# Blocks of up to 64 tokens with the high and low parts in one stationary operand, and a new order of splits around the transposes of h

## The chip, the cores and the metric

The kernel runs on one core of a Trainium2 chip. The metric is the device time of one execution in microseconds (us). TensorE (PE) multiplies matrices and transposes, VectorE (DVE) and ScalarE (ACT) work on elements, GpSimd (POOL) issues gathers and scatters, SyncE (SP) issues the other transfers. Each engine has an instruction stream of its own, and they meet at semaphores.

## The reference

Three stages follow one another; the change is in the second, which routes each of 1792 tokens to one of 8 experts:

```
def _attn_ref(q, k, v):                      # q, k, v [4, 12, 448, 64]
    scores = scale * np.matmul(q, k.transpose(0, 1, 3, 2)) - np.log(S)
    attn = 1.0 / (1.0 + np.exp(-scores))
    return np.matmul(attn, v)
def _moe_ref(x, expert_emb, tau, w1, w2):    # x [1792, 768], w1 [8, 768, 1024], w2 [8, 1024, 768]
    ...
    for e in range(E):
        mask = expert_idx == e
        h = np.maximum(x[mask] @ w1[e], 0.0)
        out[mask] = gate_w[mask, None] * (h @ w2[e])
def _moe2_ref(x, w_a, w_b, w_out):           # w_a, w_b [768, 1536], w_out [1536, 768]
    return (x @ w_a) * (x @ w_b) @ w_out
```

## The kernel before

The attention of four batches fills PE up to 208 us of the trace, the experts run from there to 545 us, and the last stage (called GLU here) to the end. Everything is float32 in and out. A float32 product is made of three products of parts: each operand is split into a high part, rounded to the narrower type that PE multiplies at full rate, and a low part, the rest; high by high, high by low and low by high are summed in PSUM.

The experts work by blocks of 128 tokens. Tables made on the chip (lines around 343) sort the tokens of two batches at a time by expert, so that there are two phases of 7 blocks each that always run, and then blocks under a condition (`live`, L983). `block(b)` reads a few flags of the next block into registers (`value`, L768): whether the expert changes (`chg`), whether weights are to be loaded (`load`), and which (`e_load`). Where an expert's tokens don't fill their last block, the rest of its rows is computed and thrown away. With this case's inputs 18 blocks do work, seven runs of one expert each with 4, 1, 3, 2, 1, 3 and 4 blocks.

What PE does in a block, in order: `p1_half` for each half `hf` of w1's columns, 6 slices of the 768 inputs by three products (`xh` with `w1h`, `xh` with `w1l`, `xl` with `w1h`, L820 to L822), 36 matmuls of 512 columns; the four transposes of each half of h (`h_tr`, L869), those of the first half inside the second `p1_half`; then 8 slices of h by three products by two halves of the output (`p2`, L906), 48 matmuls of 384 columns, with the transposes of the second half of h behind the first eight and six transposes of the next block's tokens (`x_load`, L756) behind the next four. ACT copies each product to SBUF as `h` with the Relu (L823) and makes the high parts (L760), DVE makes the low parts (L761: `hTl`, `xl`, `w1l`, `w2l`) and the scaled output `y` (L951), which POOL scatters (L957).

Where the expert changes, ACT and DVE also split the new weights under `when_new`, a condition that each of them branches on (L887): w1 in the block before (`split_new(1, 0, KD)`, all six slices behind `x_load`), w2 at that block's end and in the next. SP loads the expert's 7 MB ahead (`load_w`, L772). In the same stretch `prep_tick` makes ready the weights of the GLU: raw words from memory, a copy `ab` on ACT (L199, L201), work on POOL and DVE, and a store `wm<-ab` (L224) on SP; `ab` has three buffers, so that ACT waits there for an earlier store to land.

The order of each engine's instructions is that of the code; buffers come from pools with few tiles (`ps_x` four PSUM tiles for all transposes, `h` two).

## Time and profile before

| | |
|---|---|
| time, median of 3 runs | 1087.31 us (1085.61 to 1088.32) |
| the profiled execution: its time, its span | 1089.07 us, 1087.3 us |
| busy share of the span: PE, DVE, ACT, POOL | 98%, 55%, 46%, 14% |
| the expert stage in the trace | 208.4 to 545.1 us, 18 blocks |
| an ordinary block on PE | 18.0 to 18.1 us |

A share of busy time is a mean over stages; here PE is near full in all three, so a time is read from PE's stream: how long its instructions take, and the few places where it stands.

### The profile page before, as it was taken

What the parts mean: (1) busy time and instruction counts of PE and PEld (TensorE: products, weight loads), DVE (VectorE), ACT (ScalarE), POOL (GpSimd) and SP (SyncE); (2) the same over time, 40 slices, a digit from 0 to 9 for tenths busy, and PEclk for the clock granted to TensorE, in tenths of its full rate; (3) what the DMA queues carried; (4) which work ended last, traced back from release to release, by engine and by line L of the source; (5) the groups of instructions that cost most, each with busy time, mean ns of one, the idle gap of its engine ahead of it and who ended that gap; (6) DMA issues with size and microseconds to landing.
All of it is one profiled execution on the core that took longest, in us unless ns stands there. A gap on an engine that the chain in (4) does not pass through costs nothing.

```text
span 1087.3 us, 16743 instructions
## 1 busy us (share of the span) xinstructions
PE 1066.4 (98%) x5996; PEld 866.6 (80%) x5996; DVE 594.7 (55%) x1037; ACT 501.5 (46%) x761; POOL 152.9 (14%) x218
## 2 busy tenths in 40 slices
PE   7999999999999999999999999999999999999998
PEld 4555555589888988898978878888888888888997
DVE  2566788756792969371255996333334333333553
ACT  5777767442762767261244563332233323233543
POOL 2121322232221222231101331000000000000000
PEclk9999999899999999999999999999999999999999
DMA  6687687639659775823183764073221262220730
GB/s 164 166 214 202 178 234 215 201 110 344 230 211 342 292 254 218 312 62 130 46 285 123 254 209 174 1 290 132 87 87 44 72 273 91 87 88 1 319 132 30
DMA packets 116740, 187.65 MB, mean 173 GB/s; under 512 B 53784, under 2 KB 88856, under 8 KB 110624
## 3 DMA queue, kind: packets, MB, share of 16 engines
q1 hardware_dynamic: 112000, 171.10, 46.8%
q0 software_dynamic: 3040, 14.94, 3.7%
q8 instruction: 48, 0.79, 0.3%
q10 hardware_dynamic: 1600, 0.39, 0.2%
q14 instruction: 52, 0.43, 0.1%
HBM read 154.17 MB, written 32.24 MB: 171 GB/s over the span
## 4 chain that ended last, share of the span: by engine, by line
PE 44%; DVE 3%; DMA 2%; ACT 1%; issue 0%; POOL 0%; SPq 0%; ACTq 0%; POOLq 0%
PE ab L1075 10%; PE ab L1076 10%; PE ab L1077 10%; PE o L1108 5%; PE o L1109 5%; PE o L1110 5%; DVE wlo L761 1%; DMA wx<-wm 1%; DVE m L195 1%; DMA r<-wm 1%; PE ab L756 0%; DVE wx L212 0%; PE py L756 0%; ACT whi L760 0%; DVE m L197 0%
## 5 line engine op out<-in xcount | busy, mean ns | idle before, releaser
L1075 PE MATMUL ab<-yh,whi 128*128 128x512 f32 (+1 forms) x576 | 210.7, 366 | 2.2 <-DVE m L1083 2.1
L1076 PE MATMUL ab<-yl,whi 128*128 128x512 f32 (+1 forms) x576 | 210.0, 365 | 0.0
L1077 PE MATMUL ab<-yh,wlo 128*128 128x512 f32 (+1 forms) x576 | 209.8, 364 | 0.0
L202 POOL TENSOR_TENSOR m<-m,raw 128x384 int32<-128x384 int32 x72 | 76.5, 1063 | 366.2 <-DVE m L197 204.7
L1075 PEld LDWEIGHTS ab<-yh,whi 128*128 128x128 f32 x576 | 109.3, 190 | 18.4 <-DVE m L1083 2.6
L1077 PEld LDWEIGHTS ab<-yh,wlo 128*128 128x128 f32 x576 | 109.4, 190 | 17.5 <-DVE wlo L761 0.2
L1076 PEld LDWEIGHTS ab<-yl,whi 128*128 128x128 f32 x576 | 109.4, 190 | 15.9
L1108 PE MATMUL o<-whi,gh 128*128 128x512 f32 x336 | 114.7, 341 | 0.0
L1109 PE MATMUL o<-whi,gl 128*128 128x512 f32 x336 | 113.8, 339 | 0.0
L1110 PE MATMUL o<-wlo,gh 128*128 128x512 f32 x336 | 112.9, 336 | 0.0
L1083 DVE TENSOR_TENSOR m<-ab,a 128x512 f32<-128x512 f32 (+1 forms) x48 | 29.9, 624 | 146.5 <-PE ab L1077 146.4
L760 ACT CAST gh<-m 128x512 fp32r<-128x512 f32 (+1 forms) x48 | 27.2, 567 | 169.9 <-DVE m L1083 169.9
L557 ACT ACTIVATE a<-ps,bias_s 128x896 f32<-128x896 f32 x96 | 92.8, 1006 | 26.6 <-PE ps L552 25.9
L761 DVE TENSOR_TENSOR wlo<-wx,whi 128x768 fp32r<-128x768 f32 x72 | 65.5, 965 | 49.4 <-ACT whi L760 49.4
L761 DVE TENSOR_TENSOR wlo<-r,whi 128x768 fp32r<-128x768 f32 x70 | 65.1, 985 | 47.9 <-ACT whi L760 47.9
L820 PE MATMUL p<-w1h,xh 128*128 128x512 f32 x216 | 86.3, 399 | 0.1
L821 PE MATMUL p<-w1l,xh 128*128 128x512 f32 x216 | 84.8, 393 | 0.4 <-DVE w1l L761 0.3
L822 PE MATMUL p<-w1h,xl 128*128 128x512 f32 x216 | 84.7, 392 | 0.0
L574 PE MATMUL av<-a,v 128*64 128x448 f32 (+1 forms) x384 | 79.4, 570 | 1.6 <-DVE xtok L590 1.6
L906 PE MATMUL p<-w2h,hTh 128*128 128x384 f32 x288 | 76.5, 346 | 0.0
L760 ACT CAST whi<-wx 128x768 fp32r<-128x768 f32 x72 | 55.4, 832 | 44.2 <-PE o L1109 36.3
L760 ACT CAST whi<-r 128x768 fp32r<-128x768 f32 x70 | 53.8, 832 | 47.0 <-PE o L1109 42.5
(236 smaller groups left out, 1830.2 us busy)
## 6 DMA issues: line engine op xcount, KB each, us to landing
wx<-wm SPq DMA_DIRECT2D x22, 1152.0 KB
r<-wm SPq DMA_DIRECT2D x21, 1152.0 KB
r<-in_moe_w_dram SPq DMA_DIRECT2D x28, 768.0 KB
r<-in_moe_w_dram SPq DMA_DIRECT2D x18, 1024.0 KB
raw<-in_moe_w_a_dram SPq DMA_DIRECT2D x24, 384.0 KB
raw<-in_moe_w_b_dram SPq DMA_DIRECT2D x24, 384.0 KB
raw<-in_moe_w_out_dram SPq DMA_DIRECT2D x24, 384.0 KB
wm<-ab SPq DMA_DIRECT2D x48, 192.0 KB
```

The costliest lines, as they stand in the source:

```text
L557: nc.scalar.activation(out=a[r], in_=ps[:n, :, :S], func=AF.Sigmoid, bias=bias_s[:n], scale=qscale)
L760: nc.scalar.copy(out=hi, in_=src)
L761: eng.tensor_tensor(out=lo, in0=src, in1=f32_hi, op=ALU.subtract)
L820: nc.tensor.matmul(ps, lhsT=xh[:, kk, :], rhs=w1h[kk][:, cs], start=kk == 0, stop=False)
L821: nc.tensor.matmul(ps, lhsT=xh[:, kk, :], rhs=w1l[kk][:, cs], start=False, stop=False)
L822: nc.tensor.matmul(ps, lhsT=xl[:, kk, :], rhs=w1h[kk][:, cs], start=False, stop=kk == KD - 1)
L1075: nc.tensor.matmul(ps[:, :n], lhsT=hi[:, s, cs], rhs=yh[:, kk, :n], start=kk == 0, stop=False)
L1076: nc.tensor.matmul(ps[:, :n], lhsT=hi[:, s, cs], rhs=yl[:, kk, :n], start=False, stop=False)
L1077: nc.tensor.matmul(ps[:, :n], lhsT=lo[:, s, cs], rhs=yh[:, kk, :n], start=False, stop=kk == KD - 1)
L1108: nc.tensor.matmul(t[:, d0:d1], lhsT=gh[:, cs], rhs=hi[:, 2, d0:d1], start=first, stop=False)
L1109: nc.tensor.matmul(t[:, d0:d1], lhsT=gl[:, cs], rhs=hi[:, 2, d0:d1], start=False, stop=False)
L1110: nc.tensor.matmul(t[:, d0:d1], lhsT=gh[:, cs], rhs=lo[:, 2, d0:d1], start=False, stop=last)
```

## The change

A block gets a sixth flag, `full_of`. It is 0 for an expert's second block if the expert has at least three and its remainder is at most 64 tokens; the ranks of its tokens are moved so that the partly filled block is that second one, not the last. In such a half block the low parts of x go into columns 64 to 127 of `xh` behind the high parts of the same 64 tokens, so that one product with `w1h` and one with `w1l` do for both, and the third product is left out. Instead of transposing h on PE, a matmul with the constant `fold` (two identities above each other) sums the two halves of rows while it turns them. The split then puts the high parts of h in columns 0 to 63 of `hTl` too and uses `hTl` as the stationary operand of p2; `y` is summed from the two halves of rows. With these inputs blocks 1 (64 tokens), 6 (3 tokens) and 15 (64 tokens) are half blocks. All engines that differ branch on the flag.

In all blocks after the first: the three products of p1 run one after the other over all slices; the Relu moves from the copy of h to its split; `x_load` comes behind the whole first half of p2 and behind the split of h's second half, with two new slices of w1 split ahead of it and four behind; in the second half of p2 `hTl`'s products stand ahead of those with `w2l`.

```
+    fold = ctile([P, P], "fold")
...
+        for cs in (slice(0, P // 2), slice(P // 2, P)):
+            gp.tensor_tensor(out=fold[:, cs], in0=ident[:, :P // 2], in1=ident[:, P // 2:], op=ALU.add)
...
+        over = st("over", [P, E2])
+        ve.scalar_tensor_tensor(out=over, in0=nb, scalar=-float(P), in1=run, op0=ALU.mult, op1=ALU.add)
...
+        ve.scalar_tensor_tensor(out=over, in0=nb, scalar=-float(P), in1=run, op0=ALU.mult, op1=ALU.add)
+        po = st("po", [CP, MAXC, E], tag="py")[:, :n_c, :]
+        gp.tensor_tensor(out=po, in0=oh_all[:, c0:c1, :],
+                         in1=over[:CP, ph * E:(ph + 1) * E].unsqueeze(1).to_broadcast([CP, n_c, E]), op=ALU.mult)
+        yield
+        yield
+        ov = st("ov", [CP, MAXC], tag="pr")[:, :n_c]
+        ve.tensor_reduce(out=ov, in_=po, axis=AX.X, op=ALU.add)
+        rq = st("rq", [CP, MAXC], tag="bk")[:, :n_c]
+        ve.tensor_tensor(out=rq, in0=rk_all[:, c0:c1], in1=ov, op=ALU.subtract)
+        ve.scalar_tensor_tensor(out=ov, in0=rq, scalar=2.0 * P, in1=ov, op0=ALU.is_ge, op1=ALU.mult)
+        ve.tensor_tensor(out=rq, in0=rk_all[:, c0:c1], in1=ov, op=ALU.subtract)
         ri = st("ri", [CP, MAXC], I32)[:, :n_c]
-        ve.tensor_copy(out=ri, in_=rk_all[:, c0:c1])
+        ve.tensor_copy(out=ri, in_=rq)
...
+        fw = st("fw", [1, E2])
+        ve.tensor_scalar(out=fw, in0=over[0:1], scalar1=-float(P // 2), scalar2=None, op0=ALU.is_le)
+        ve.scalar_tensor_tensor(out=fw, in0=nb[0:1], scalar=3.0, in1=fw, op0=ALU.is_ge, op1=ALU.mult)
+        ve.scalar_tensor_tensor(out=fw, in0=beg[0:1], scalar=2.0, in1=fw, op0=ALU.add, op1=ALU.mult)
...
+        ve.tensor_scalar(out=flg[ph][:, 5, :n_t], in0=hb_, scalar1=-1.0, scalar2=1.0, op0=ALU.mult, op1=ALU.add)
...
+    def either(b, whole, half, who=1):
+        if b not in full_of:
+            whole()
+            return
+        with tc.If(full_of[b][who] == 1) as c:
+            whole()
+        with c.Else():
+            half()
+
+    def x_high(b, hf, px):
+        n = KD // 2
+        src = px[:, :n * P].rearrange("p (k c) -> p k c", k=n)
+        nc.scalar.copy(out=xs_t[b % 2][0][:, hf * n:(hf + 1) * n, :], in_=src)
+        return src
+
+    def x_low(b, srcs):
         xh, xl = xs_t[b % 2]
         n = KD // 2
-        ks = slice(hf * n, (hf + 1) * n)
-        split(xh[:, ks, :], xl[:, ks, :], px[:, :n * P].rearrange("p (k c) -> p k c", k=n), xh[:, ks, :].bitcast(F32))
+
+        def low(o, cs, os):
+            for hf, src in enumerate(srcs):
+                ks = slice(hf * n, (hf + 1) * n)
+                nc.vector.tensor_tensor(out=o[:, ks, os], in0=src[:, :, cs], in1=xh[:, ks, cs].bitcast(F32),
+                                        op=ALU.subtract)
+
+        either(b, lambda: low(xl, slice(0, P), slice(0, P)), lambda: low(xh, slice(0, PH), slice(PH, P)), 2)
...
+            x_low(b, [x_high(b, hf, pxs[hf]) for hf in range(2)])
...
+    def when_full(b, whole, half=None, again=True):
+        if b not in full_of:
+            whole()
+            return
+        with tc.If(full_of[b][0] == 1, label=f"full{b}_{n_full[0]}", preferred_fallthrough_block=True) as c:
+            whole()
+        if half is not None:
+            with c.Else():
+                half()
+        n_full[0] += 1
+        if again:
+            hint(b)
...
+        if b in full_of:
+            def run_over(l, wv, first=False, last=False):
+                for kk in range(KD):
+                    nc.tensor.matmul(ps, lhsT=l[:, kk, :], rhs=wv[kk][:, cs], start=first and kk == 0,
+                                     stop=last and kk == KD - 1)
+
+            run_over(xh, w1h, first=True)
+            if hf == 0:
+                when_full(b, lambda: run_over(xl, w1h))
+            else:
+                px = misc["ps"]()
+
+                def whole():
+                    run_over(xl, w1h)
+                    h_turn(b, 0, px, False)
+
+                when_full(b, whole, lambda: h_turn(b, 0, px, True))
+                h_split(b, 0, px)
+                inner()
+            run_over(xh, w1l, last=True)
...
-        nc.scalar.activation(out=h, in_=ps, func=AF.Relu)
+        nc.scalar.copy(out=h, in_=ps)
...
+    def h_turn(b, hf, px, half):
+        for kk in range(FH // P):
+            cs = slice(kk * P, (kk + 1) * P)
+            if half:
+                nc.tensor.matmul(px[:, cs], lhsT=hs_of[b][hf][:, cs], rhs=fold, start=True, stop=True)
+            else:
+                nc.tensor.transpose(out=px[:, cs], in_=hs_of[b][hf][:, cs], identity=ident)
+
+    def h_split(b, hf, px):
+        n = FH // P
+        hi, lo = (hT[nm][:, hf * n:(hf + 1) * n, :] for nm in "hl")
+        src = px.rearrange("p (k c) -> p k c", k=n)
+        nc.scalar.activation(out=hi, in_=src, func=AF.Relu)
+        nc.vector.scalar_tensor_tensor(out=lo, in0=src, scalar=0.0, in1=hi.bitcast(F32), op0=ALU.max,
+                                       op1=ALU.subtract)
+        if b in full_of:
+            with tc.If(full_of[b][3] == 0):
+                nc.scalar.activation(out=lo[:, :, :PH], in_=src[:, :, :PH], func=AF.Relu)
...
+            def half1(yp, px, half):
+                a = hTl if half else hTh
+                p2(yp, 0, 2, ((a, w2h), (a, w2l)))
+                h_turn(b, 1, px, half)
+
+            def half1b(yp, half):
+                a = hTl if half else hTh
+                p2(yp, 2, KF // 2, ((a, w2h), (a, w2l)))
+                if not half:
+                    p2(yp, 0, KF // 2, ((hTl, w2h),))
+
+            def half2(yp, half):
+                a = hTl if half else hTh
+                p2(yp, KF // 2, KF, ((a, w2h),))
+                if not half:
+                    p2(yp, KF // 2, KF, ((hTl, w2h),))
+                p2(yp, KF // 2, KF, ((a, w2l),))
...
-            p2(yp, 0, 2, slice(0, 2))
-            h_tr(b, 1)
-            p2(yp, 2, 3, slice(0, 2))
+            px = misc["ps"]()
+            when_full(b, lambda: half1(yp, px, False), lambda: half1(yp, px, True))
+            when_full(b, lambda: half1b(yp, False), lambda: half1b(yp, True))
+            h_split(b, 1, px)
+            if b > 0:
+                when_new(lambda: split_new(1, 0, 2))
+            else:
+                split_new(2, 4, KF)
             x_load(b + 1)
             if b == 0:
-                split_new(2, 4, KF)
                 when_new(lambda: load_new(1), load)
                 when_new(lambda: load_new(2), load)
-            when_new(lambda: split_new(1, 0, KD))
-            p2(yp, 3, KF // 2, slice(0, 2))
-            p2(yp, 0, KF // 2, slice(2, 3))
+            when_new(lambda: split_new(1, 2 if b > 0 else 0, KD))
             gather(b + 2)
             tick()
             if 0 < b < LIVE - 1:
                 prep_tick(behind=1)
-            p2(yp, KF // 2, KF, slice(0, 2))
-            p2(yp, KF // 2, KF, slice(2, 3))
+            when_full(b, lambda: half2(yp, False), lambda: half2(yp, True), False)
...
+            def y_half():
+                gt = slots[:, 2, b:b + 1]
+                for hf in range(2):
+                    yo = y[:, hf * HD:(hf + 1) * HD]
+                    nc.scalar.activation(out=yo, in_=yp[hf][:, :HD], func=AF.Copy, scale=gt)
+                    nc.vector.scalar_tensor_tensor(out=yo[:PH], in0=yp[hf][PH:, :HD], scalar=gt[:PH], in1=yo[:PH],
+                                                   op0=ALU.mult, op1=ALU.add)
+
+            either(b, y_whole, y_half)
...
+                full_of[nx] = [value(nx, 5, 1, es) for es in ([ET.PE], [ET.Activation, ET.DVE], [ET.DVE], [ET.Activation])]
```

The order on the engines, at three places of blocks 5 and 6, both in the unrolled code (every block has the same rows). PE in the second `p1_half` of block 5, around the transposes of the first half of h; `p_...` is the accumulator, `xh` and `xl` the parts of the tokens. Before:

```order
L820 MATMUL p_4176<-w1h_123,xh_116 128x512
L821 MATMUL p_4176<-w1l_129,xh_116 128x512
L822 MATMUL p_4176<-w1h_123,xl_117 128x512
L869 MATMUL px<-ident,h 128x128 x4
L820 MATMUL p_4176<-w1h_124,xh_116 128x512
L821 MATMUL p_4176<-w1l_130,xh_116 128x512
```

And with the change:

```order
L888 MATMUL p_4721<-w1h_125,xl_118 128x512
L888 MATMUL p_4721<-w1h_126,xl_118 128x512
L959 MATMUL px<-ident,h 128x128 x4
L873 UNCONDITIONAL_BRANCH
L957 MATMUL px<-fold,h 128x128 x4
L873 UNCONDITIONAL_BRANCH
L989 UNCONDITIONAL_BRANCH
L888 MATMUL p_4721<-w1l_127,xh_117 128x512
```

The transposes stand behind twelve of eighteen matmuls as they did, but what follows them is the six with `w1l`; a full block jumps over the matmuls with `fold`, a half block comes to them with neither the six `xl` products nor the transposes.

ACT from the end of block 5 to the copy of h in block 6 (`flg` holds the flags, `r` the loaded weights). Before:

```order
L201 ACTIVATE ab<-raw 128x384
L887 COMPARE_AND_BRANCH
L760 CAST w2h_2790<-r_2921 128x768
L760 CAST w2h_2791<-r_2921 128x768
L760 CAST w2h_2792<-r_2921 128x768
L760 CAST w2h_2793<-r_2921 128x768
L887 UNCONDITIONAL_BRANCH x2
L768 TENSOR_LOAD flg_105
L768 ISA x2
L823 ACTIVATE h<-p_4368 128x512
```

And with the change:

```order
L1085 ACTIVATE y<-p_4778,slots 128x384
L1085 ACTIVATE y<-p_4779,slots 128x384
L820 UNCONDITIONAL_BRANCH
L989 COMPARE_AND_BRANCH
L784 CAST w2h_2812<-r_2943 128x768
L784 CAST w2h_2813<-r_2943 128x768
L784 CAST w2h_2814<-r_2943 128x768
L784 CAST w2h_2815<-r_2943 128x768
L989 UNCONDITIONAL_BRANCH x2
L792 TENSOR_LOAD flg_106
L792 ISA x2
```

Here the last two rows stand three times before the copy of h comes; ahead of them is a branch around the two `y` operations of a half block.

ACT behind the second half of h in block 5. Before:

```order
L201 ACTIVATE ab<-raw 128x384
L760 CAST hTh<-px 128x512
L760 CAST xh_114<-px 128x384 x2
L887 COMPARE_AND_BRANCH
L760 CAST w1h_120<-r_0_118 128x1024
```

And with the change:

```order
L965 ACTIVATE hTh<-px 128x512
L969 COMPARE_AND_BRANCH
L970 ACTIVATE hTl<-px 128x4x64
L969 UNCONDITIONAL_BRANCH x2
L989 COMPARE_AND_BRANCH
L784 CAST w1h_121<-r_0_119 128x1024
L784 CAST w1h_122<-r_0_119 128x1024
L989 UNCONDITIONAL_BRANCH x2
L828 CAST xh_115<-px 128x384 x2
```

A half block's copy into `hTl` (L970) follows the high part, and the tokens' high parts come behind two slices of w1.

## Rows read from the trace of the kernel before

**Rows 1.** The page: busy time by engine, and the chain that ended last.

```profile
PE 1066.4 (98%) x5996; PEld 866.6 (80%) x5996; DVE 594.7 (55%) x1037; ACT 501.5 (46%) x761; POOL 152.9 (14%) x218
...
PE 44%; DVE 3%; DMA 2%; ACT 1%; issue 0%; POOL 0%; SPq 0%; ACTq 0%; POOLq 0%
```

**Rows 2.** Windows, blocks 6, 7, 11, 14: busy time, PE clock, DMA share, GB/s.

```profile
325.10:343.10 18.00, 18.00 (x100) 16.40 (x99) 6.39 (x12) 4.58 (x9) 4.76 (x5) 1.00 1.01 378
...
343.10:362.30 19.20, 18.15 (x99) 16.26 (x98) 9.53 (x13) 10.16 (x15) 3.12 (x4) 1.00 0.58 205
...
416.60:436.80 20.20, 19.20 (x100) 16.04 (x99) 18.80 (x27) 11.89 (x21) 5.31 (x5) 1.00 0.38 128
...
472.80:490.90 18.10, 18.10 (x99) 16.33 (x99) 13.44 (x19) 9.18 (x15) 7.69 (x2) 1.00 0.31 102
```

**Rows 3.** Timeline of PE in block 15: start us, us, engine, line.

```profile
497.55 0.39 PE L822 MATMUL p<-w1h,xl 128*128 128x512 f32 x1
497.78 0.60 PE L869 MATMUL px<-ident,h 128*128 128x128 f32 x4
498.13 0.48 PE L820 MATMUL p<-w1h,xh 128*128 128x512 f32 x1
...
502.17 0.63 PE L756 MATMUL px<-ident_r,xg 128*128 128x128 f32 x6
...
503.40 1.55 PE L906 MATMUL p<-w2h,hTl 128*128 128x384 f32 x8
504.79 0.51 PE L906 MATMUL p<-w2h,hTh 128*128 128x384 f32 x2
```

**Rows 4.** Timeline of PE, plain float32 matmuls of 84 columns.

```profile
267.49 1.02 PE L427 MATMUL px<-hotb,hotp 112*128 112x84 f32 x8
268.30 0.47 PE L820 MATMUL p<-w1h,xh 128*128 128x512 f32 x1
```

**Rows 5.** Timeline of PE at the end of the expert stage.

```profile
545.83 0.42 PE L756 MATMUL py<-ident_r,raw 128*128 128x128 f32 x3 [0.70 <-PEq L983]
```

**Rows 6.** Timeline of ACT in block 15.

```profile
498.46 0.59 ACT L760 CAST hTh<-px 128x512 fp32r<-128x512 f32 x1 [2.55 <-PE px L869]
```

**Rows 7.** Timeline of DVE in block 15.

```profile
499.08 0.69 DVE L761 TENSOR_TENSOR hTl<-px,hTh 128x512 fp32r<-128x512 f32 x1 [6.98 <-ACTq L887]
```

**Rows 8.** Timeline of SP in blocks 6 and 7.

```profile
325.07 1.88 SPq L772 DMA_DIRECT2D r<-in_moe_w_dram  x3
...
340.57 0.34 SPq L224 DMA_DIRECT2D wm<-ab  x1
```

**Rows 9.** Timeline of all engines in block 7.

```profile
349.12 0.55 ACT L201 ACTIVATE ab<-raw 128x384 f32<-128x384 bf16 x1 [9.08 <-DMA wm<-ab]
...
350.48 0.60 ACT L823 ACTIVATE h<-p 128x512 f32<-128x512 f32 x1 [0.82 <-ACTq L887]
...
351.13 0.66 PE L869 MATMUL px<-ident,h 128*128 128x128 f32 x4 [1.05 <-ACTq L887]
```

**Rows 10.** Timeline of ACT in block 9.

```profile
384.99 0.55 ACT L201 ACTIVATE ab<-raw 128x384 f32<-128x384 bf16 x1 [8.83 <-DMA wm<-ab]
386.28 0.60 ACT L823 ACTIVATE h<-p 128x512 f32<-128x512 f32 x1 [0.74 <-ACTq L887]
```

**Rows 11.** Timeline of PE in block 9.

```profile
387.29 0.60 PE L869 MATMUL px<-ident,h 128*128 128x128 f32 x4
```

**Rows 12.** Source line L768, register loads: ns min/median/max, first and last start.

```profile
L768 ACTq TENSOR_LOAD <-flg x23: 272/279/557, 220.6 to 522.4; - x23
...
L768 ACTq FUSED_REGOPS  x18: 147/147/173, 221.2 to 522.2; - x18
```

**Rows 13.** Source line L887, branches of the expert's change.

```profile
L887 ACTq COMPARE_BRANCH  x94: 34/40/141, 224.8 to 539.6; - x94
```

**Rows 14.** Source line L983, branches of the conditional blocks.

```profile
L983 PEldq COMPARE_BRANCH  x6: 63/82/375, 469.7 to 545.5; - x6
```

**Rows 15.** Timeline of DVE in block 5.

```profile
302.80 6.92 DVE L761 TENSOR_TENSOR w1l<-r,w1h 128x1024 fp32r<-128x1024 f32 x6
```

More of the change, by code (lines that the diff above doesn't have):

```diff
@@ L353, in tables @@
         ve.tensor_copy(out=rpf, in_=rp)
-        yield
-        yield
         cum = st("cum", [P, E2])
@@ L804, in x_load, with hint @@
             transpose_raw(pxs[hf], t, hf * n, n)
-            if not first:
-                x_split(b, hf, pxs[hf])
-        for hf in range(2):
-            if first:
-                x_split(b, hf, pxs[hf])
+        if first:
+            for hf in range(2):
+                src = x_high(b, hf, pxs[hf])
+                ks = slice(hf * n, (hf + 1) * n)
+                nc.vector.tensor_tensor(out=xl[:, ks, :], in0=src, in1=xh[:, ks, :].bitcast(F32), op=ALU.subtract)
+        else:
+            x_low(b, [x_high(b, hf, pxs[hf]) for hf in range(2)])
         xT_[b] = (xh, xl)
     e_of, hs_of = {}, {}
+    def hint(b):
+        tc.mark_branch_hint_location(f"full{b}_{n_full[0]}", full_of[b][0], [ET.PE])
+    n_full = [0]
+    def when_full(b, whole, half=None, again=True):
[10 more added lines that the diff above has]
+            hint(b)
     def p1_half(b, hf, ps, h, inner, at=4):
@@ L900, in p1, with p2 @@
                         mx_p.tile([P, FH], F32, tag="h", name="h"), inner)
[L902 removed]
+            def p2(yp, k0, k1, parts):
                 for kk in range(k0, k1):
[L904 removed]
+                    for i, (l, wv) in enumerate(parts):
                         for hf in range(2):
                             nc.tensor.matmul(yp[hf][:, :HD], lhsT=l[:, kk, :], rhs=wv[kk][:, hf * HD:(hf + 1) * HD],
[L907 to L908 removed]
+                                             start=kk == 0 and i == 0 and len(parts) == 2,
+                                             stop=kk == KF - 1 and wv is w2l)
+            def half1(yp, px, half):
[13 more added lines that the diff above has]
+                p2(yp, KF // 2, KF, ((a, w2l),))
             def tick():
```

51 lines of the change are left out of this document (27 added, 24 removed).

## The prediction

> **What bounds the kernel now.** I read the page first: PE is busy 98% of the span and heads the chain that ended last [rows 1]. Next the windows, one for each block [rows 2]: in an ordinary block PE is busy the whole time, 18.00 of 18.00 us in block 6, at a granted clock of 1.00, while DVE and ACT work a third of it. So what a block costs is the sum of PE's matmuls, and a matmul taken out of a block shortens it, unless what PE then comes to sooner isn't there yet. The windows also show where PE stands already: block 7 takes 19.20 us with 18.15 busy, block 11 20.20 with 19.20. The timeline of block 7 shows what the first of these is [rows 9]: PE waited 1.05 us to turn h's first half, since ACT had sat 9.08 us until a store `wm<-ab` had landed, then made `ab` at 349.12, read its registers and copied h at 350.48, so that PE could begin at 351.13 only. This is where I expect part of the gain to be lost. The rest of what I read are prices.
>
> **What a half block leaves out.** On PE two 512-column matmuls start 0.23 us apart (497.55, 497.78), and eight of 384 columns take 504.79 - 503.40 = 1.39 us, 0.174 each [rows 3]. A half block loses 12 matmuls with `xl`, 12 x 0.23 = 2.75 us, and 16 with `hTl` in p2, 16 x 0.174 = 2.78, together 5.5 us.
>
> **What it adds on PE.** Four transposes and what they delay come to 0.45 us: they start at 497.78, the next matmul at 498.13, and that one takes 0.48 where others take 0.39 [rows 3]. A turn with `fold` is a plain float32 matmul; four such, of 84 columns, stand as eight passes from 267.49 to 268.30, 0.81 us [rows 4]. With 128 columns I take 0.9, twice in a block, so +0.9 over the transposes. (Lower end 0.7, at 0.81 a turn; upper end 1.6, if the passes grow with the columns, 0.81 x 128/84 = 1.23.)
>
> **Waits of the half block.** Before `hTl` can be the stationary operand three steps must follow the turn: ACT's high part (498.46, 0.59 us) [rows 6], DVE's low part (499.08, ended 499.77) [rows 7], and ACT's copy of the high half into `hTl`, which no row shows. It has half the elements of a 0.59 us operation; I estimate 0.35 (between nothing but its hand-over, 0.05, and 0.59). From the turn's end at 498.38 [rows 3] to 499.77 + 0.35 and about 0.1 of hand-overs are 1.85 us, and two conditions on ACT are ahead of the copy, each a branch of 0.04 us [rows 13], and a wait of ACT for its own last operation, so I take 2.1. In the first half only six matmuls with `w1l` cover it, 6 x 0.23 = 1.4 us, less what the turn still takes: PE stands 0.8 (0.4 to 1.1). In the second, eight matmuls (1.39) and `x_load`'s six transposes (502.17; half as much again as four, 0.5 or more [rows 3]) do: 0.3 (0 to 0.6). PE's jump from p1 to the first turn also makes it stand. The only taken jump on PE in the trace is the exit of the conditional blocks, where it stood 0.70 us [rows 5], its sequencer's own part at most 0.375 [rows 14]; I take 0.35 (0 to 0.7).
>
> So block 15 gains 5.5 - 0.9 - 1.1 - 0.35 = 3.15 us. Block 1 has the same sum, but about 1 us of small table matmuls lies among its own and covers a part of the first wait: 3.3.
>
> **Block 6's gain is not kept.** It is 3.15 us too, and block 7 follows. The store on which ACT sat had been issued at 340.57, with the expert's loads issued from 325.07 on ahead of it [rows 8], in a block in which the DMA engines were full, share 1.03 [rows 2]. The loads start at block 6's beginning, which its own length doesn't move, so the store still lands at about 349.05. Before block 7 ACT also has two more registers to read, 0.28 + 0.15 us each [rows 12], and a branch around `y` with its jump, together about 1.2 to 1.45 us, all between `ab` and h's copy (in the order shown above they stand just there). So h is turned at about 352.4 where it was at 351.13: block 6's 3.15 are gone and 1.3 more. A little of it is made good by an earlier start of block 6 (below): blocks 5 to 7 together +1.0. Both ends: if the store lands by as much earlier as block 6 is shorter, this term is -2.0 instead; if ACT's extra work is longer, +2.
>
> **Block 9.** The same waiting, without a half block: `ab` 384.99, h's copy 386.28 [rows 10], ends 386.88, and PE turns h at 387.29, not late yet [rows 11]. There are 0.4 us to spare, and ACT's extra 1.3 comes on top: +0.9 (0 to 1.4). In the other blocks ACT comes to h's copy earlier than PE wants it by more than this: nothing there.
>
> **New order in full blocks.** Where the expert changes, the low parts of w1 are what PE comes to too soon: six of them take DVE 6.92 us in one piece [rows 15] in block 5, and block 11, the other of its kind, takes 20.20 us against 18.10 in block 14 [rows 2]. With all `xh` by `w1h` first, then `xl`, the first `w1l` is wanted 12 matmuls (2.7 us) later but all six then in one row, and DVE has two slices done ahead of the tokens: -0.5 for the two blocks (-1.5 to +0.5). The tokens' parts come 2.1 us later (12 matmuls by 0.174), of some 9 us that they have: nothing, unless ACT and DVE are as full as in those blocks, which is the upper end.
>
> **Branches on PE in full blocks.** Each has five compares and four jumps over at most 26 instructions. A compare on PE takes 0.06 to 0.08 us of its sequencer [rows 14], on ACT 0.04 [rows 13], the jumps among them at most 0.141. PE's sequencer is about 3 us ahead of its matmuls (the compare ahead of block 14 is at 469.7 [rows 14], that block begins at 472.80 [rows 2]), so a delay of this size is made good before a matmul is late: +0.5 for all 14 blocks, for stops that don't quite fit. The low end is 0. What it costs if that cover is gone is the slower rival.
>
> The extra table operations (ten small ones on DVE and POOL) lie beside PE's work in blocks 0 to 6; attention and GLU keep their instructions: 0.
>
> **The sum.** -3.15 - 3.3 + 1.0 + 0.9 - 0.5 + 0.5 = -4.5 us. The profiled execution took 1089.07 us and so would come to 1084.5; the median of the runs is 1.76 lower, and from it 1087.31 - 4.5 = 1082.8, my forecast.
>
> **The rivals.** *Jumps on PE are paid for (slower).* If the sequencer isn't ahead at a jump, because the jump empties what it had read, every one costs between half and all of the 0.375 us of [rows 14]. 14 full blocks with 4 jumps are 56, +10.5 to +21 us on -5.0: 1093 to 1103. For it speaks the exit, where PE stood 0.70 [rows 5]; against it that the exit leads far, and that these lead over few instructions. The sum turns to slower than now at 5.0/56 = 0.09 us a jump. The Trainium skill, "Runtime: NRT & Kernel Launch", section "Instruction fetch mechanics", says that a taken branch whose target is outside the fetched pages waits for a DMA fetch; jumps over 26 instructions mostly stay within, so by it the sum would be the one without its +0.5, 1082.3. No row here shows which jumps leave the pages.
>
> *Block 6's gain is kept.* The store lands earlier, or another transfer's order lets ACT go: -4.5 - 3.0 = -7.5, 1079.8. For it: less traffic may stand ahead of it; against it the DMA share of 1.03, which leaves no room.
>
> *Nothing is left.* What block 1 gains is lost where a later block waits for a store or for weights, as block 6's is: -4.5 + 3.3 = -1.2, 1086.1; with the waits, the jump and the turns of block 15 at their upper ends too (0.3 + 0.3 + 0.35 + 0.7 = 1.65 more) it is 1087.8. For it: blocks 2 to 5 lie under the same transfers; against it: PE has no wait of a microsecond in them now.
>
> **How the numbers follow.** The sum 0.5; block 6 kept 0.17; nothing left 0.18; jumps paid 0.15. The likeliest alone reaches from 1080.5 to 1086 (turns and waits ±1, order ±1, ACT's extra ±1). The range 1079 to 1091 takes in all but the jumps and the lowest part of block 6 kept, some 0.2. 0.3%, about what a measurement of this kernel can tell from no change, is 3.3 us: faster means below 1084.05. Of the sum 0.31 lies there and 0.19 within, block 6 kept lies below, nothing left within, and of the jumps 0.13 lie above 1090.6 and 0.02 within: faster 0.48, same 0.39, slower 0.13.
>
> **What will show it.** The windows of blocks 1, 6 and 15 should show about 15 us, with 1 to 1.5 of PE idle, waiting in PE's waits for ACT at the first `hTl` product. Block 7 should grow to about 23 us, its transposes waiting for ACT, and block 9 by 0.9. An ordinary full block (8, 12, 16) should stay at 18.0 to 18.1; if it is 18.2 or more, jumps are paid and the forecast fails. If block 7 stays at 19 us, block 6's gain was kept; if blocks 2 to 4 grow by 3 us, block 1's was lost. A block 11 above 20.2 would put the order of the splits wrong.

## The result and the profile after

The changed kernel takes 1094.74 us (1092.48 to 1095.58, 6 runs) beside 1087.82 of the kernel before on the same chip: ratio 1.0066, with a 95% interval of 1.005 to 1.0082. It is slower by 7 us; I had forecast 4.5 us faster, and the time is outside my range. The profiled execution is its fastest, 1092.48 us with a span of 1090.8, and that of the kernel before, 1089.07 us, is slower than all six runs timed here, so the traces show 3.5 us of the 7.

The page after, busy time. PE works 10.3 us less than before [rows 1] in a longer span.

```profile
PE 1056.1 (97%) x5936; PEld 855.6 (78%) x5936; DVE 601.4 (55%) x1059; ACT 508.4 (47%) x773; POOL 155.0 (14%) x222
```

The windows of blocks 1, 2, 5, 6, 7, 9, 13 and 15 of the kernel after, columns as in [rows 2]:

```profile
228.91:244.47 15.56, 15.05 (x89) 13.42 (x89) 8.33 (x30) 6.13 (x13) 4.32 (x9) 1.00 0.22 63
244.47:265.20 20.73, 19.32 (x107) 17.29 (x107) 16.94 (x57) 5.76 (x11) 6.82 (x11) 1.00 1.03 398
...
303.20:323.95 20.75, 19.36 (x98) 16.30 (x99) 19.15 (x28) 12.09 (x21) 4.02 (x4) 1.00 0.34 118
323.95:345.96 22.01, 16.49 (x79) 14.65 (x79) 6.50 (x12) 5.44 (x11) 5.01 (x5) 0.85 1.01 377
345.96:364.65 18.69, 18.37 (x100) 16.48 (x99) 9.27 (x13) 11.19 (x17) 3.78 (x3) 0.99 0.42 136
...
383.19:401.20 18.01, 18.01 (x99) 16.43 (x99) 9.14 (x13) 10.13 (x15) 4.44 (x4) 1.00 0.48 164
...
457.94:477.04 19.10, 18.24 (x99) 16.36 (x99) 7.82 (x10) 9.21 (x13) 3.33 (x3) 1.00 0.22 80
...
495.60:510.50 14.90, 14.08 (x80) 12.24 (x80) 3.55 (x6) 4.00 (x8) 1.95 (x2) 1.00 0.37 127
```

Blocks 1 and 15 gave 3.4 and 3.1 us (they take 15.56 and 14.90). Block 6, half as well, takes 22.01 us of which PE works 16.49, at a clock of 0.85; before it took 18.00 [rows 2]. Ordinary blocks such as 9 stay at 18.01. Between them blocks 2, 5 and 13 grew by 1.9, 1.1 and 1.1, and 4, 8, 10 and 14 by 0.4 to 0.8. The stage (from the first matmul of block 0 to the last of block 17) took 338.9 us instead of 336.4, and the GLU behind it 540.15 instead of 538.27.

The waits of PE from block 0 to the end of the stage, us in total, how many, the longest (a name with `q` is an engine's sequencer, which takes branches, register loads and semaphores):

```profile
PE p L1008 <- ACTq L989: 6.3, 4, 4.8
...
PE px L959 <- ACT h L911: 1.8, 6, 0.3
PE p L1008 <- DVEq L989: 1.5, 3, 1.0
PE p L888 <- DVE w1l L785: 1.3, 2, 0.6
PE px L959 <- ACTq L989: 1.2, 2, 0.9
```

These name ACT or DVE, none PE's own sequencer; left out are the attention's, those at the way out, and two of 0.4 us and less. The largest is at the first `hTl` product of a half block. The timeline of ACT in block 6 shows it, and PE's row there:

```profile
331.61 0.59 ACT L911 COPY h<-p 128x512 f32<-128x512 f32 x1 [0.18 <-ACTq L989]
...
338.39 0.54 ACT L204 ACTIVATE ab<-raw 128x384 f32<-128x384 bf16 x1 [5.75 <-DMA wm<-ab]
338.84 0.58 ACT L965 ACTIVATE hTh<-px 128x512 fp32r<-128x512 f32 x1
340.24 0.38 ACT L970 ACTIVATE hTl<-px 128x256 fp32r<-128x256 f32 x1 [0.82 <-DVEq L989]
```

```profile
340.68 1.33 PE L1008 MATMUL p<-w2h,hTl 128*128 128x384 f32 x3 [4.79 <-ACTq L989]
```

ACT copied h's second half at 331.61, then stood 5.75 us behind the store `wm<-ab` with the next `ab`, and split h at 338.84 only; DVE's low part and the copy into `hTl` (L970) followed, and PE had stood 4.79 us. PE's clock there, in windows of 4 us:

```profile
336.00:340.00 4.00, 0.00 (x0) 0.00 (x0) 0.54 (x1) 1.03 (x2) 0.98 (x1) 0.92 1.04 403
340.00:344.00 4.00, 3.32 (x10) 3.33 (x11) 2.59 (x6) 1.80 (x4) 0.00 (x0) 0.50 1.03 403
344.00:348.00 4.00, 4.00 (x16) 3.65 (x16) 0.05 (x1) 0.00 (x0) 1.02 (x1) 0.73 0.85 308
348.00:352.00 4.00, 4.00 (x19) 3.31 (x18) 1.15 (x2) 1.61 (x3) 0.00 (x0) 1.00 0.45 143
```

By the means of these rows the granted clock is 0.50, the lower of the two levels (1.2 GHz), from about 339.4, while PE still stands, until about 346.2. PE's work from 340.7 on, 5.5 us, goes at half speed there: an estimated 2.8 us lost behind the 4.8.

The same comes once more at the way out of the stage. Timeline of the first products and parts of the GLU:

```profile
548.55 1.69 ACT L784 CAST yh<-py 128x384 fp32r<-128x384 f32 x4 [5.46 <-DVEq L1119]
...
551.25 1.95 DVE L785 TENSOR_TENSOR yl<-py,yh 128x384 fp32r<-128x384 f32 x4 [3.56 <-ACT whi L784]
...
552.89 0.76 PE L1212 MATMUL ab<-yh,whi 128*128 128x512 f32 x1 [2.41 <-DVE yl L785]
```

```profile
550.00:552.00 2.00, 0.48 (x6) 0.34 (x4) 0.75 (x2) 2.00 (x6) 0.00 (x0) 0.75 0.93 333
552.00:554.00 2.00, 1.11 (x3) 0.85 (x4) 2.00 (x5) 2.00 (x5) 0.00 (x0) 0.50 1.06 439
554.00:556.00 2.00, 2.00 (x6) 1.56 (x6) 2.00 (x6) 0.13 (x1) 0.00 (x0) 0.50 0.94 355
556.00:558.00 2.00, 2.00 (x6) 1.57 (x5) 2.00 (x5) 1.67 (x3) 0.00 (x0) 0.54 1.11 375
```

ACT's `yh` begins at 548.55 and DVE's last branch out of the conditional blocks is at 548.6, but its first `yl` is at 551.25. PE works 1.6 us of the four from 550 to 554, and the clock is at its lower level from about 551 to 558. Before, too, PE stood at its exit [rows 5], but not for the first `yl`, and its clock fell as well, for half as long:

```profile
548.00:550.00 2.00, 2.00 (x14) 1.77 (x12) 2.00 (x5) 2.00 (x6) 0.00 (x0) 0.50 0.79 181
550.00:552.00 2.00, 2.00 (x7) 1.51 (x7) 2.00 (x6) 1.90 (x5) 0.00 (x0) 0.65 1.07 433
```

### The profile page after: what moved, and what is told of

Its sections match the earlier page's. It is cut to its first block, busy times and chain, and to the rows that moved or that the text cites. A ratio compares the mean times of both kernels' runs of the same rounds, so it can differ in the third digit from the quotient of the medians.

```text
span 1090.8 us, 17515 instructions
## 1 busy us (share of the span) xinstructions
PE 1056.1 (97%) x5936; PEld 855.6 (78%) x5936; DVE 601.4 (55%) x1059; ACT 508.4 (47%) x773; POOL 155.0 (14%) x222
## 4 chain that ended last, share of the span: by engine, by line
PE 43%; DVE 3%; DMA 2%; ACT 1%; issue 1%; POOL 0%; SPq 0%; ACTq 0%; DVEq 0%; POOLq 0%
PE ab L1212 10%; PE ab L1213 10%; PE ab L1214 10%; PE o L1245 5%; PE o L1246 5%; PE o L1247 5%; DMA wx<-wm 1%; DVE wlo L785 1%; DVE m L198 1%; DMA r<-wm 1%; PE ab L780 0%; DVE wx L215 0%; ACT whi L784 0%; DVE m L200 0%; POOL m L205 0%
## 5 line engine op out<-in xcount | busy, mean ns | idle before, releaser
L1214 PEld LDWEIGHTS ab<-yh,wlo 128*128 128x128 f32 x576 | 109.3, 190 | 17.5 <-DVE wlo L785 0.2
L784 ACT CAST whi<-wx 128x768 fp32r<-128x768 f32 x72 | 55.3, 832 | 41.9 <-PE o L1246 35.4
L1245 PEld LDWEIGHTS o<-whi,gh 128*128 128x128 f32 x336 | 63.4, 189 | 8.2
L1246 PEld LDWEIGHTS o<-whi,gl 128*128 128x128 f32 x336 | 63.5, 189 | 7.4
L1247 PEld LDWEIGHTS o<-wlo,gh 128*128 128x128 f32 x336 | 63.2, 188 | 7.4
L1008 PE MATMUL p<-w2h,hTl 128*128 128x384 f32 x288 | 59.8, 344 | 8.1 <-ACTq L989 6.3
```

The source lines that it names most:

```text
L784: nc.scalar.copy(out=hi, in_=src)
L1008: nc.tensor.matmul(yp[hf][:, :HD], lhsT=l[:, kk, :], rhs=wv[kk][:, hf * HD:(hf + 1) * HD], start=kk == 0 and i == 0 and len(parts) == 2, s ...
L1214: nc.tensor.matmul(ps[:, :n], lhsT=lo[:, s, cs], rhs=yh[:, kk, :n], start=False, stop=kk == KD - 1)
L1245: nc.tensor.matmul(t[:, d0:d1], lhsT=gh[:, cs], rhs=hi[:, 2, d0:d1], start=first, stop=False)
L1246: nc.tensor.matmul(t[:, d0:d1], lhsT=gl[:, cs], rhs=hi[:, 2, d0:d1], start=False, stop=False)
L1247: nc.tensor.matmul(t[:, d0:d1], lhsT=gh[:, cs], rhs=lo[:, 2, d0:d1], start=False, stop=last)
```

## The experiments

The kernel before was timed again beside each group of runs and came to between 1085.46 and 1087.82 us. Kernels of different groups are therefore compared by what each takes over its own before; the kernel after takes 6.9 us over it.

**What the parts cost: all blocks whole, and the order alone.**

```diff
 # all_full
-        ve.tensor_scalar(out=flg[ph][:, 5, :n_t], in0=hb_, scalar1=-1.0, ...
+        ve.tensor_scalar(out=flg[ph][:, 5, :n_t], in0=hb_, scalar1=0.0, ...
```

> The sixth flag is always 1: every block is computed whole, with all branches, register loads and table operations of the change; nothing of the output changes. Theory A (the full blocks pay on ACT's and DVE's queues: register loads, conditions, later operands): the time is that of the change plus the work that blocks 1 and 15 had saved (3.4 + 3.1 us) less the wait of 4.8 us and the slower blocks 6 and 7 (3.4 us over before): about +3 to +5, 1097.5 to 1100 us, PE's waits naming ACT and DVE, and an ordinary block such as 9, 12, 16 still 18.0 us. Theory B (PE pays at its own branches): the same total, but ordinary blocks at 18.3 us or more. Theory C (the half blocks themselves lose, by their waits): it is no slower than the change, 1093 to 1095 us or less.

1099.43 us, ratio 1.0117 (1.0098 to 1.0137). An ordinary block is 18.00 to 18.04, so theory B falls: PE's branches cost nothing that shows. The stage is 345.07 us, 8.7 over before, in blocks 2, 4 to 8, 10, 13 and 14, and PE's waits there are for ACT and DVE. Theory C falls as well: the half blocks bring something, 6.2 us in the stage, 7.1 by the times over before (14.0 here). But not all of it is kept. The window of block 2 here:

```profile
250.09:269.18 19.09, 19.06 (x108) 17.32 (x107) 15.32 (x54) 4.70 (x9) 5.57 (x9) 1.00 1.03 399
```

Behind a whole block 1, block 2 takes 19.09 us; behind the half block it takes 20.73. So 1.6 of the 3.4 us that block 1 gives come back there. Blocks 6 and 7 take 41.9 us here and 40.7 in the kernel after: what block 6 leaves out brings 1.2.

```diff
 # order_only: no flag, no condition, no register load, the tables of before
-        with tc.If(full_of[b][0] == 1, ...) as c:
-            whole()
+        whole()
...
-                full_of[nx] = [value(nx, 5, 1, es) for es in ...]
+                full_of[nx] = True
```

> The new order of p1, of the splits and of p2 in all blocks, but no flag, no branch, no register load, no half block, and the tables of before; nothing of the output changes. Theory A (register loads and conditions make ACT and DVE late): about the time of before, 1086.5 to 1089 us, blocks 4, 8, 10 at 18.1 and block 13 at 18.0. Theory D (the new order itself is late where weights change): 1090 us or more, with blocks 5 and 11 at 20.5 us and blocks 4, 8, 10, 14 at 18.4 or more, waiting for h's copy.

1091.40 us, ratio 1.005 (1.0031 to 1.0069), 5.9 over its before: slower, so by its time theory D seemed right, but its blocks say no. Blocks 4, 8, 10 and 14 are at 18.14, 13 at 18.02 and the stage at 336.79, before 336.4; blocks 5 to 7 are together 1.2 longer, 0 and 11 shorter. What its trace shows lost is mostly in the GLU, 539.39 us or 1.1 more, where PE waits 2.0 us for the first `yl` as in the kernel after. The conditions and register loads then are what makes blocks 8, 10, 13 and 14 longer in all_full.

**The way out of the blocks.** Idle DVE operations in the code of a block that never runs:

```diff
 # dve_pad
             either(b, y_whole, y_half)
+            if b == NBLK - 1:
+                for _ in range(64):
+                    nc.vector.memset(y[:, 0:1], 0.0)
```

> The change, with 64 tiny DVE operations added to the code of the last conditional block, which never runs here: they only move where the code that follows lies. Theory E (DVE stands 2.1 us at its jump out of the conditional blocks because the code it leads to isn't there yet, which depends on where it lies): the standing before the first yl changes, to 0.2 us or to another place, and the time with it by up to 2 us, 1092.5 to 1095 us. Rival F (DVE waits there for data): the 2.1 us stay, whatever the code's place.

1090.06 us (12 runs), ratio to before 1.0032 (1.002 to 1.0045): 3.7 us over its before where the kernel after takes 6.9, so 3.2 less, though no instruction that runs is different. I had expected 2 at most. Timeline of DVE and of PE there, and a window at its clock:

```profile
550.26 1.95 DVE L785 TENSOR_TENSOR yl<-py,yh 128x384 fp32r<-128x384 f32 x4 [1.58 <-ACT yh L784]
```

```profile
551.89 0.48 PE L1215 MATMUL ab<-yh,whi 128*128 128x512 f32 x1 [0.42 <-DVE yl L785]
```

```profile
552.00:554.00 2.00, 2.00 (x7) 1.28 (x8) 2.00 (x6) 2.00 (x7) 0.00 (x0) 1.00 1.09 433
```

The standing before the first product is 0.42 us instead of 2.41, the clock stays at its upper level, and the GLU takes 536.75 us, 3.4 less: 2.0 of standing, and I put the rest down to the half clock. Rival F falls. Three more kernels tried to say which place is bad:

```diff
 # before_pad: the same loop with range(125) in the kernel before
 # order_pad: range(3) in order_only;  order_pad64: range(64) in it
```

> The kernel before, with 125 tiny DVE operations added to the code of its last conditional block, which never runs here; they move the code that follows on DVE to the place that it has in order_only (instruction 2255 of its stream, not 2130). Theory E (the place of code costs the time at the jump out of the conditional blocks): DVE stands some 2 us between its last jump and the first yl, and the time is 2 to 4 us above before, 1088.5 to 1090.5 us, without a change in any block. Rival F: nothing changes, within 0.5 us of before.

1087.54 us, ratio 1.0005 (0.9992 to 1.0019), 0.40 us of standing: theory E in this form is wrong. The place in DVE's own stream isn't what decides; the rest of the program differs between the two kernels, and so may where the code lies.

> order_only with 3 tiny DVE operations added to the code of the last conditional block, which never runs; the code behind it then lies where it does in the kernel before modulo 128 instructions. Theory E: the 2.2 us of standing before the first yl are gone, the time is 2 to 4 us below order_only, 1087 to 1089.5 us. Theory D (the new order itself costs what order_only lost): unchanged, 1090 to 1092 us.

1091.16 us, 2.03 us of standing, GLU 539.41: as order_only, so theory E fails here too; the time is that of theory D, the blocks are not.

> order_only with 64 tiny DVE operations in the code of the last conditional block, which never runs. If what order_only loses (1091.4) is the standing of 2.0 us at the way out of the blocks and the half clock after it, and 64 operations move it away as they did in dve_pad: no standing over 0.5 us before the GLU's first product, the stage 336.5 to 337 us, the time 1086 to 1088.5 us, that of before. If the new order of p1 and the splits costs by itself: 1090 to 1092 us with the standing gone. If 64 operations don't move it here: the standing of 2 us is seen again and the time is 1090.5 to 1092.

The standing is gone, GLU 538.22, yet 1089.88 us, ratio 1.0028 (1.0016 to 1.0041). Its stage is 336.82. Over their own before order_only takes 5.9 us, order_pad 3.6 and this one 3.1: with the standing went between 0.5 and 2.8 us. The first two differ by three operations that never run, both stand, and yet lie 2.4 us apart, so a difference of 2 us between groups shows little. Of the 3.1 that stay, the stage shows 0.4; the rest is open (below).

**Register loads.**

```diff
 # loads_behind: chg, live and full are read here, no longer ahead of the block
                 p1(0, lambda: None)
+                got = flags()
```

> The change, with the register loads of the flags (the expert's change, live, full) put behind the copy of h's first half of a block instead of ahead of it; nothing of the output changes. Theory A3 (register loads on ACT between a late ab and the copy of h cost time): block 13's wait of 0.86 us and some of block 7's go and ACT stands less before h; 1 to 3 us less than the change, 1092 to 1094 us. Rival: the loads are hidden but for block 13, and the time is within 0.5 us of the change; or they now delay the split of h's first half, and it is slower by 1 us or more.

1093.69 us, ratio 1.0071 (1.0053 to 1.009), 8.2 over its before, so no gain: block 13 came back to 18.03 and 7 to 18.03, but 5, 8, 10, 14 and 15 grew by 0.4 to 1.5. Both theory and rival have a part: the moved loads are late for something else. Its block 6 shows another cost, on PE's timeline:

```profile
329.13 1.30 PE L888 MATMUL p<-w1h,xh 128*128 128x512 f32 x5
335.35 0.98 PE L957 MATMUL px<-fold,h 128*128 128x128 f32 x3 [4.92 <-issue]
```

At the jump of a half block to its first `fold` PE stood 4.92 us for nothing that the profile shows ("issue"), h having been copied long before (ACT, 329.16 to 329.75). In the half blocks of the kernel after it doesn't stand at this jump.

```diff
 # one_flag: ACT and DVE take a block as half where chg is 2
+        ve.scalar_tensor_tensor(out=flg[ph][:, 1, :n_t], in0=hb_, scalar=2.0, in1=c0_[:, :n_t], ...
...
-                full_of[nx] = [value(nx, 5, 1, es) for es in ([ET.PE], [ET.Activation, ET.DVE], ...)]
+                full_of[nx] = [value(nx, 5, 1, [ET.PE]), chg]
```

> The change, with the half block told by the value 2 of the flag of the expert's change, so that ACT and DVE read one register for each block as before, not three; nothing of the output changes. Theory A3 (register loads on ACT and DVE cost time where ACT is late): block 13 back to 18.0 to 18.3 us, block 7 1 us shorter, block 2 0.4 shorter; 2 to 3.5 us less than the change, 1091 to 1093 us. Rival A4 (the conditions around h's split and y cost it, not the loads): within 1 us of the change, with the 0.3 us waits for h's copy in blocks 4, 8, 10, 14 as they are. Both keep those waits unless the loads cause them.

1088.83 us, ratio 1.002 (1.0007 to 1.0033). Rows of the kernel after, of ACT in block 13 and of the register loads on it, and ACT in block 13 here:

```profile
461.22 0.54 ACT L204 ACTIVATE ab<-raw 128x384 f32<-128x384 bf16 x1 [5.97 <-DMA wm<-ab]
465.16 0.59 ACT L911 COPY h<-p 128x512 f32<-128x512 f32 x1 [3.40 <-issue]
...
L792 ACTq TENSOR_LOAD <-flg x59: 272/277/539, 219.8 to 527.8; - x59
```

```profile
461.15 0.55 ACT L204 ACTIVATE ab<-raw 128x384 f32<-128x384 bf16 x1 [5.92 <-DMA wm<-ab]
463.11 0.59 ACT L912 COPY h<-p 128x512 f32<-128x512 f32 x1 [1.41 <-PE p L889]
```

With 59 loads on ACT (23 before [rows 12]) h was copied 3.9 us after `ab`, with one flag 2.0, and block 13 is at 18.01: theory A3. Blocks 8, 10 and 14 stay at 18.5 to 18.7, so those 0.4 us belong to the conditions, as A4 has it. one_flag takes 2.5 us over its before. The standing at the way out is 0.40 here too, as in dve_pad, which was timed in the same group and takes 3.7: so 1.2 us of the time are left for the loads. The stage is 335.6, 3.2 less than in the kernel after, 1.1 of it in block 13 and the most, 1.4, in block 6, where PE still stands 4.2 us. Which of the two sizes is right is not shown.

**ACT behind the store.**

```diff
 # ab_late: store, product and load of each unit where they were (prep_ahead), its operations later:
 # the first unit's behind split_new(1, 2, KD), the second's behind p1(0)
-                    prep_tick(behind=1)
+                    prep_ahead(behind=1)
...
+            if 0 < b < LIVE - 1:
+                prep_unit()
```

> The change, with the operations of each unit of the GLU's weights put later in the code: the first unit of a block behind the tokens and the slices of w1, the second behind the next block's copy of h's first half; the transfers stay where they are, nothing of the output changes. Theory A1 (block 6's gain is lost because ACT stands before h's split, waiting for a store to land): PE's wait of 4.8 us in block 6 goes, block 6 takes 16 to 17.5 us and block 7 at most 20; the whole 3 to 5 us less than the change, 1090 to 1092 us. Rival A2 (block 6 would wait for something else then, the tokens of block 7 or the y of block 5): blocks 6 and 7 together still 40 us, the time within 1 us of the change.

1115.02 us, ratio 1.0269. Block 6 came to 14.87, below the 16 to 17.5 of theory A1, but 5, 7, 9 and 11 took 24 to 26.5: ACT stands behind the store all the same, now ahead of the split of h's first half, and PE stood 5.8 and 5.9 us in blocks 7 and 9. At this place the wait costs more than where it was. So it was taken off ACT:

```diff
 # ab_pool (ab_pool6: in block 6 alone)
-        nc.scalar.activation(out=ab, in_=t16, func=AF.Abs)
+        nc.gpsimd.tensor_tensor(out=ab, in0=t16, in1=t16, op=ALU.mult)
...
-            ... in0=ab, scalar=1.125 * 2.0 ** -15, ...
+            ... in0=ab, scalar=1.265625 * 2.0 ** -30, ...
```

> The change, with the operation that makes ab moved from ACT to POOL (the square of the word instead of its size, with the squared threshold behind it; nothing of the output changes), so that POOL and not ACT waits for the stores to land. Theory A1 (block 6's gain and more is lost since ACT stands behind a store): blocks 6 and 7 without a wait of over 1 us, together about 34 us (15 and 18 to 19) instead of 40.7, block 13 still at 19.1 or a little less; the whole 5 to 7 us less than the change, 1087 to 1090 us. Rival A2 (the DMA queues themselves bound blocks 5 to 7, by the weights or the tokens): 39 to 41 us for the two, within 1 us of the change.

1104.15 us: blocks 6 and 7 did as A1 says, 14.79 and 18.03, but POOL made `ab` everywhere: blocks 2, 5, 8 and 11 took 21.3 to 22.3 us, and the GLU 551.3, with PE waiting twice for some 4.6 us for `m`. So only in block 6:

> The change with ab on POOL in block 6 alone, all else as it is (three register loads, ACT's copy behind DVE's low parts, the way out of the blocks with its standing of 2 us). Theory A1: blocks 6 and 7 together 32.5 to 34 us instead of 40.7, no half clock in them; block 8 takes 1 to 2.5 us more, since weights land no sooner; 5 to 6.5 us less than the change, 1088 to 1090 us. Rival A2: what block 6 gives comes back in blocks 7 to 11 as a whole, 1092 us or more.

1087.17 us, ratio 1.0 (0.999 to 1.0011): 0.4 over its before, 6.5 less than the kernel after. Windows of blocks 6 to 9:

```profile
325.23:340.09 14.86, 14.10 (x79) 12.25 (x79) 6.05 (x11) 5.00 (x10) 3.31 (x4) 1.00 1.01 367
340.09:358.13 18.04, 18.04 (x99) 16.44 (x99) 10.31 (x14) 9.46 (x15) 7.80 (x7) 1.00 0.77 279
358.13:377.46 19.33, 18.79 (x99) 16.27 (x99) 18.61 (x27) 12.89 (x21) 4.15 (x4) 1.00 0.96 369
377.46:396.82 19.36, 18.25 (x100) 16.37 (x99) 9.19 (x14) 10.13 (x15) 4.80 (x4) 1.00 0.52 177
```

14.86 and 18.04 at full clock: 32.9 us instead of 40.7. Blocks 8 and 9 take 0.8 and 1.3 more, and the stage 333.2, 5.6 less. A1 holds; the standing at the way out (2.1 us) is still there.

**Together.**

```diff
 # combo, best1: one_flag, 64 idle operations, ab on POOL (best1: in block 6), and in a half block
-        ... with tc.If(full_of[b][3] == 0):  ACT: lo[:, :, :PH] behind DVE's lo
+        ... ACT: lo[:, :, :PH] beside DVE's lo[:, :, PH:]
 # best2: also
-                p1(1, rest)
+                p1(1, lambda: None)
+                when_new(lambda: split_new(2, KF - 2, KF), was_new)
```

> The change with ab on POOL, one flag for ACT and DVE, the half block's high parts copied by ACT beside DVE's low parts instead of behind them, and the 64 idle operations. Theory A (all losses of the change stand on ACT's and DVE's queues): blocks 1, 6 and 15 at 14.2 to 15 us, 7 and 13 at 18.1; the stage 326 to 330 us instead of 338.9, the time 1080 to 1084 us, below that before the change. Rival D (the order of p1 and the splits costs by itself, blocks 4, 5, 8, 10, 14): those stay 0.4 to 1 us above before, and the time is 1083 to 1087 us.

1098.66 us, where theory A had 1080 to 1084: its GLU is 548.6, nearly as long as ab_pool's, and the stage 334.7 instead of 326 to 330. Blocks 1, 6 and 15 came to 14.2 to 14.9 and 7 and 13 to 18.03, as expected, but 2, 5, 8 and 11 take over 21, as in ab_pool.

> The change with one flag for ACT and DVE, the half block's high parts copied by ACT beside DVE's low parts, ab on POOL only in block 6, and the 64 idle operations. Theory A with E (all losses are on ACT's and DVE's queues and at the exit): blocks 6 and 7 together 32 to 33 us, 8 at 18.6, 1 and 15 at 14.3 to 14.9; the stage 329 to 332 us, the time 1080 to 1084 us, below before. Rival (what block 6 gives comes back in block 8 and 11, since weights and stores land no sooner): the stage 334 us or more, 1085 to 1088 us.

1081.40 us (1081.07 to 1083.11), ratio 0.9951 (0.9932 to 0.997): faster than both kernels. Windows of blocks 1, 6, 7, 8 and 15:

```profile
231.46:246.31 14.85, 14.70 (x90) 13.32 (x89) 7.89 (x31) 5.89 (x13) 4.38 (x10) 1.00 0.23 64
...
323.90:338.17 14.27, 13.92 (x80) 12.25 (x79) 5.60 (x12) 4.80 (x10) 2.01 (x2) 1.00 0.99 353
338.17:356.88 18.71, 18.23 (x99) 16.39 (x99) 7.30 (x12) 8.33 (x14) 7.64 (x8) 1.00 0.81 298
356.88:377.06 20.18, 18.97 (x100) 16.29 (x100) 19.35 (x28) 14.00 (x22) 4.15 (x4) 1.00 0.99 357
...
488.65:502.91 14.26, 13.92 (x80) 12.25 (x79) 3.01 (x6) 3.78 (x8) 1.95 (x2) 1.00 0.37 129
```

Blocks 1, 6 and 15 are at 14.3 to 14.9; the stage is 328.84. The rival has its share: block 8 takes 20.18, 2 us more than before.

> best1 with the last two slices of w2 split behind the copy of h's second half instead of ahead of it. Theory G (PE's 0.3 us waits for that copy in blocks 4, 5, 8, 10, 11, 14 come from ACT being late by its conditions behind these splits): the waits go, the blocks 8, 10, 14 come to 18.1 us, 1.5 to 2.5 us less than best1. Rival: the split of h's second half is then late by as much, and nothing changes or it is slower by up to 2 us.

1081.68 us, within 0.3 of best1. Blocks 4, 8, 10 and 14 are 18.20, 20.19, 18.28 and 18.03 (best1: 18.49, 20.17, 18.53, 18.55), so theory G is right for 4, 10 and 14, not for 8, and 5 and 11 grew by 0.2 to 0.3; the stage is 1.5 us shorter, but its GLU is 538.60 with two stretches at half clock where best1 has 536.54 with none, and the time doesn't show it.

```diff
 # best1_full: best1 with scalar1=0.0 in flag row 5, scalar=0.0 in flag row 1
```

> best1 with the flag of half blocks always off, so that every block is computed whole. What the half blocks bring once ACT isn't in their way is the difference to best1 (1081.4): by PE's matmuls three times 3.7 to 4.2 us, less 2 us that come back in block 8, so 1090.5 to 1093 us. Theory A: the branches that stay (PE's, ACT's, DVE's) cost full blocks 2 to 4 us over the kernel before, in blocks 2, 4, 5, 8, 10, 14. Rival: the half blocks' gain is worth 6 us or less since most comes back in blocks that wait for weights: 1087.5 us or less.

1089.21 us, ratio 1.0019 (1.0009 to 1.0029), a little below what I gave: 2.4 over its before, where best1 is 6.2 below its own. Once nothing is in their way, the half blocks are worth 7.8 us in the stage (336.62 to 328.84: 11.7 in the three blocks, less 3.9 that come back in 2, 7, 8 and 9) and 8.6 by the times. Blocks 2, 4, 5, 8, 10 and 14 are together 2.2 longer than before, as theory A has it; but 0, 7 and 11 are 2.1 shorter, so the stage is as long as before, and the 2.4 us of the time don't show there.

## Why the prediction was wrong

PE in block 15 of the kernel after, around the first turn:

```profile
498.76 1.52 PE L888 MATMUL p<-w1h,xh 128*128 128x512 f32 x6
500.12 1.05 PE L957 MATMUL px<-fold,h 128*128 128x128 f32 x8
500.93 1.62 PE L888 MATMUL p<-w1l,xh 128*128 128x512 f32 x6
...
503.12 0.62 PE L1008 MATMUL p<-w2h,hTl 128*128 128x384 f32 x2 [0.57 <-ACTq L989]
```

- **What a half block leaves out and adds**: right, but the close figure is luck in part. Block 15 gave 3.12 us where I had 3.15, block 1 3.44 where I had 3.3. The copy into `hTl` takes 0.38 us (I had 0.35). The turn takes 0.81 us (I had 0.9), PE doesn't stand at the jump ahead of it (I had 0.35) and 0.57 at the first `hTl` product (0.8). By the window of the block PE stood 0.8 us in it where I had 1.45, and worked 14.1, only 3.9 less than before where I had 4.6: two misses that cancel.
- **"Block 6's gain is not kept", blocks 5 to 7 together +1.0**: the mechanism was right, the place and the size were not. I had ACT's wait for the store delay block 7's first turn; it delayed block 6's own second split, on which with the change PE waits for three steps, not one. And I left out that PE then runs at half clock. Blocks 6 and 7 cost 3.4 us over before and 5 another 1.1: +4.6. ab_pool6 shows the cause: with that wait off ACT blocks 6 and 7 take 7.8 us less, and 6.5 of it stay in the time. It isn't the half block alone: where block 6 is whole, PE waits 1.0 us (all_full) and 1.5 us (order_only) for the same split, and in all_full 2.9 us for block 7's first turn, the place I had named.
- **"In the other blocks ACT comes to h's copy earlier than PE wants it: nothing there"**: this step failed. I priced ACT's extra loads and conditions only where I had seen ACT late. Blocks 2, 4, 8, 10, 13 and 14 grew by 5.1 us together: 13 by loads (one_flag), 8, 10 and 14 by conditions. In 2, the one with the tables, which I had at 0, DVE is late with h's low parts (1.0 us), and by all_full this is mostly block 1's gain coming back. So my rival "nothing is left" has a share: I gave 3 us in blocks 2 to 4 as its sign, and they grew by 2.8. Block 9, where I had +0.9, didn't change.
- **New order, -0.5**: not found. In order_only and order_pad64 blocks 5 to 7 are 1.2 us longer, 0 and 11 together 1.0 shorter; the stage comes to +0.4.
- **Branches on PE, +0.5**: less than that, and the slower rival (jumps on PE) didn't come: blocks 9, 12, 16 stay at 18.01. The chance of "slower" that I gave rested on these jumps alone, so that it came out slower is no merit of it. One jump in loads_behind did cost 4.9 us.
- **"GLU keep their instructions: 0"**: they do, and yet it is 1.9 us longer in the trace; dve_pad takes 3.2 us off the time with nothing but idle code. The 1.9 is the less since the profiled execution of before had two stretches at half clock behind the stage, one here and one at 650 us: before_pad, which runs the same instructions, had none in its trace and a GLU of 536.5. I had read the exit [rows 5] as PE's price for a jump and not asked what DVE's would be.

So of the sum, -6.45 for blocks 1 and 15 came as -6.56; the rest, +1.9 in my sum, was 9.7 in the stage (less 0.7 in block 0) and 1.9 behind it; the attention ended 0.9 earlier. Its two large parts are removed by ab_pool6 (6.5 us of the time) and dve_pad (3.2 us), each alone.

**Open**: what decides whether DVE stands at the way out. It stood some 2 us in the kernel after, all_full, order_only, order_pad, loads_behind, ab_pool and ab_pool6, and not in before, before_pad, dve_pad, order_pad64, one_flag, combo, best1, best1_full and best2; in ab_late DVE didn't stand, but PE did, 2.46 us ("issue"). That code still has to be fetched there was argued, not shown: the traces list two transfers of instructions in the 2.16 us behind DVE's last branch in order_only, where it stood, and two in the same stretch of order_pad64, where it didn't. The Trainium skill, "Runtime: NRT & Kernel Launch", section "Instruction fetch mechanics", has a taken branch to a page outside the fetched ones wait for a transfer. That idle code moves the wait would fit it, and no run here shows that fetch. Open too are about 2.7 us of order_pad64 over before that its stage doesn't show; executions differ by stretches at half clock (none, one or two behind the stage), and the profiled one of before had two.

## What to carry to other kernels

Work saved on the engine that is full shortens its time only where the engines that feed it are ahead by more than what the change adds to them: count every register load, condition and copy on their queues at each place where they meet, not only at those where they are late already, and ask which in-order engine stands behind a transfer there. A wait on PE can cost more than its length: behind the one of 4.8 us the clock was at half, for an estimated 2.8 us more. And run a second build whose code merely lies elsewhere, each with the kernel before timed beside it, before a difference of a few us is put down to a change.
